# Fewer, wider vector operations, twelve conversion blocks moved forward, and five buffers for split weights in a chunk-attention, expert and MLP kernel

## The chip, the core and the metric

The kernel runs on one core of a Trainium2 chip. Its metric is the device time of one execution in microseconds (us). TensorE is written PE, VectorE DVE, ScalarE ACT, GpSimd POOL and SyncE SP; SP does no arithmetic here and issues all the DMAs, in one queue, in program order.

## The reference, cut to what matters

```python
x = attention over chunks of 64 tokens            # 2304 tokens x 512
P = softmax-like gate of x, 8 Sinkhorn rounds     # 2304 x 8
for e in range(8):                                # experts: 512 -> 1024 -> 512
    h = np.maximum(x @ w1[e], 0.0)
    out += P[:, e:e + 1] * (h @ w2[e])
h = x @ w_in                                      # MLP: 512 -> 2048 -> 512
g = h * np.clip(h + 3.0, 0.0, 6.0) / 6.0
return g @ w_out
```

`w_in` and `w_out` are float64. All else is float32, and the result is wanted in float32 accuracy.

## The kernel before, in words

Each float32 operand is split in two parts, `hi` and `lo` (ACT copies `hi`, POOL subtracts it to leave `lo`), and each product is three PE products: hi·hi, hi·lo, lo·hi. A split is called a **cut** here (`cut_piece`, L804 for ACT and L805 for POOL).

**Phase one** (until 276 us of the profile) holds the attention, the gate and expert 0. It runs over 48 steps (6 blocks of tokens by 8 blocks of hidden units). Each step has four places, called hooks below, at which side work is put into the program (`add(step, hook, ...)`).

**Phase two** holds experts 1 to 7 and the MLP, as two more experts. Its products use a Strassen-like scheme of seven products of half-size blocks in place of eight. The scheme needs sums of the four blocks of each weight matrix. `w1_sum` (L787) and `w2_sum` (L800) make them on DVE, as four operations of 128x256 each, in SBUF; `park_diff`, `x2_diff` and `diff` make such sums of tokens and hidden values. Phase two runs over 108 *slots* of seven *steps* each, a slot being one pair of blocks of hidden units for 768 tokens:

- slots 0 to 27 (276 to 764 us): the first 768 tokens through experts 1 to 7. Here each slot's weights are read, summed and cut for the first time, and the cut parts are stored in DRAM (`wsc`) for the other tokens.
- slots 28 to 83: the other 1536 tokens, with weights read back from `wsc` (`w1_load`, `w2r_load`).
- slots 84 to 107: the MLP. Its weights have to be summed, cut and stored beforehand. `ahead_cut` (cut) and `ahead_keep` (store) do this in two stretches of 56 cuts each, 885 to 1095 us (planned over 87 steps) and 1420 to 1625 us, and `x2_get`, `x2_scale`, `x2_add`, `x2_diff`, `x2_cut`, `x2_keep` prepare the tokens that enter the MLP.

Before all that, `w_in` and `w_out` are turned from float64 into float32 by integer operations, in 32 blocks of 128x512: `cv_load`, seven operations `cv_op` (five on DVE, two on ACT) and `cv_keep`. Before the change the first 23 blocks lie in slots 0 to 27 and 9 in later slots.

In every step the PE does one product into one of three PSUM tiles `ha`, `hb`, `hc`. A product that adds to a tile which has just been read has to wait for the reader: DVE (`u`, `p`: L925) or ACT (`p`: L929). So a late DVE or ACT stops the PE, at most two or three steps later.

What stands in which step is decided while the program is built. `book` puts an operation into the first step in which estimated engine loads (the numbers `dve=`, `act=`, `pool=`) leave room. Every engine executes its operations strictly in that order.

The buffer `m` (one tile per partition row, 4608 floats, reached by `part(offset, size)`) serves in turn for the conversion, for the MLP's weights and for its tokens. In it the cut weights of `ahead_cut` have two places, used by turns:

```python
w = part(2048 + n % 2 * 512, 512, F32R).rearrange("p (a n) -> p a n", a=2)
```

Of the kernel before, what the change touches and what calls it, by code (L numbers as in the profile page):

```python
# [28 lines left out]
def chunk_attention_moe_mlp(  # L29
# [23 lines left out]
    nc = tc.nc  # L53
# [118 lines left out]
    cv_in = {}  # L172
# [6 lines left out]
    def cv_load(i, o):  # L179
        src, _, r, c = cv_list[i]  # L180
        t = part(o, 2 * CW, U32)
        nc.sync.dma_start(
            out=t,
            in_=src.bitcast(U32)[r * 128:(r + 1) * 128, 2 * c * CW:2 * (c + 1) * CW],
        )
        cv_in[i] = t.rearrange("p (n a) -> p n a", a=2)

    CV_COST = (0.5, 0.7, 0.7, 1.1, 0.75, 0.9, 0.9)

    def cv_op(i, n, o):  # L190
        t = cv_in[i]
        lw, hw = t[:, :, 0], t[:, :, 1]
        kx = part(o + 2 * CW, CW, U32)
# [23 lines left out]
    def cv_keep(i, o):  # L217
        _, dst, r, c = cv_list[i]
        nc.sync.dma_start(
            out=dst[r * 128:(r + 1) * 128, c * CW:(c + 1) * CW], in_=part(o + 2 * CW, CW)  # L220
        )
# [216 lines left out]

    def att_x(u):
        t, hh = u  # L440
        ps = at.pop(u)["ps"]
        j, o = divmod(t * 128, NP)
        for c in range(2):
# [251 lines left out]
    PRODUCTS = {1: (1, 0), 2: (2, 1), 3: (6, 2), 4: (0, 6), 5: (3, 3), 6: (4, 4), 7: (5, 5)}  # L695
# [86 lines left out]

    def w1_sum(k, n):
        t = raw1[k]
        o, x, y, op = ((4, 0, 1, ALU.add), (5, 4, 2, ALU.subtract), (6, 2, 0, ALU.subtract),
                       (7, 3, 5, ALU.subtract))[n]
        nc.vector.tensor_tensor(out=t[:, o], in0=t[:, x], in1=t[:, y], op=op)  # L787

    def w2_sum(k, n):
        r = raw2[k]  # L790
        if n == 0:
            if k < NEXP:
                raw2[k, "s"] = pools["sum2"].tile([128, 4, 256], F32, tag="s2", name=f"s2_{k}")
            else:
                raw2[k, "s"] = r[:, 4:8]
        t = raw2[k, "s"]
        A11, A12, A22, A21 = [r[:, o] for o in range(4)]
        o, x, y, op = ((0, A21, A22, ALU.add), (1, t[:, 0], A11, ALU.subtract),
                       (2, A11, A21, ALU.subtract), (3, A12, t[:, 1], ALU.subtract))[n]
# [170 lines left out]
    def h_turned(s, r):  # L970
# [19 lines left out]
        elif r == 6:  # L990
            gate(s, t["p1"], t["p1"], 0)
            first(3)
            put(s, 2, t["p1"])
            squash(s, t["u2"])
        elif r == 7:
            gate(s, t["u2"], t["u2"], 1)
            diff(s, 5, t["t1"], t["u2"], t["t1"])
        elif r == 8:
            diff(s, 7, t["u2"], t["u3"], t["u2"])
        elif r == 9:  # L1000
            diff(s, 6, t["u3"], t["u3"], t["t1"])
# [45 lines left out]
    MW = {1: 4, 2: 5, 3: 3, 4: 6, 5: 0, 6: 1, 7: 2}  # L1047
# [178 lines left out]
    def x2_diff(kl, n):  # L1226
        a, b, c, d = x2t[kl]
        o, x, y = ((b, a, b), (a, c, a), (c, c, b), (d, d, c))[n]
        nc.vector.tensor_tensor(out=o, in0=x, in1=y, op=ALU.subtract)


    def x2_get(p, kl):
        nc.sync.dma_start(
            out=part(0, 2 * NP), in_=xraw[p][:, kl].rearrange("p i j n -> p (i j n)")
        )
        nc.sync.dma_start(
# [4 lines left out]
        a = xf_tiles(0)  # L1241
        x2t[kl] = [a[1], a[0], a[3], a[2]]
# [32 lines left out]
    with tc.manual_schedule():  # L1275
# [12 lines left out]
        opened("x01", "x0", 1, "left")  # L1288
        for p in range(NPAIR):
            xhi[p] = pools[f"x{p}"].tile([128, KD, NP], F32R, tag="xh", name=f"xh{p}")  # L1290
            xlo[p] = pools[f"x{p}"].tile([128, KD, NP], F32R, tag="xl", name=f"xl{p}")
# [130 lines left out]

        def to_right():
# [19 lines left out]
        for n in range(4):  # L1443
# [141 lines left out]
        for s in slots[:TURN]:  # L1585
# [5 lines left out]
            for n in range(4):  # L1591
                g = book(g, w2_sum, s.k, n, dve=0.7)
# [23 lines left out]
        def book_cv(g, todo, bases, pace):  # L1616
            n = len(bases)
            back = [g] * n
            for c, i in enumerate(todo):
                o = bases[c % n]  # L1620
                at_slot(0, back[c % n], cv_load, i, o)
                t = g = max(g, back[c % n] + 4)
                for x, cost in enumerate(CV_COST):
                    act = x in (1, 2)
                    g = book(g, cv_op, i, x, o, dve=cost * (not act), act=cost * act)
                at_slot(0, g + 1, cv_keep, i, o)
                back[c % n] = g + 1
                g = max(g, t + pace)
            return g + 2

        CV1 = 23
        g = book_cv(4, list(range(CV1)), (0, 3 * CW, 6 * CW), 8)
# [17 lines left out]
        def book_ahead(g, todo):  # L1650
# [4 lines left out]
            for u, (k, m) in enumerate(units):  # L1655
                plain, sums = ((0, 1, 2), (3, 4, 5, 6)) if m == 1 else ((4, 5, 6), (0, 1, 2, 3))
                h = g
                for n in range(4):
                    h = book(h, w1_sum if m == 1 else w2_sum, k, n, dve=0.65)
                for n, o in enumerate(plain + sums):  # L1660
                    if n == 3:
                        g = max(g, h + 1)
                        if u + 1 < len(units):
                            fetch(max(g, h + 1), *units[u + 1])
# [99 lines left out]
```

## Time and profile before

| what | value |
|---|---|
| median of 3 runs | 2030.87 us (2024.29 to 2033.15) |
| the profiled execution's own time | 2026.22 us |
| its span, first to last instruction | 2024.4 us |
| mean granted clock of the PE | 0.985 of full speed |
| PE busy | 1926.4 us, 95% of the span |
| DVE busy | 1618.5 us, 80% |
| POOL busy | 1238.4 us, 61% |
| ACT busy | 813.7 us, 40% |

The span is 1.8 us shorter than the execution's own time, which holds the start and the end around it. The profiled execution lies near the lower end of the runs. A granted clock of 1.00 is the PE's 2.4 GHz and 0.5 is 1.2 GHz; a mean between them says for how long the lower one was granted.

### The profile page before, as it was taken

The numbers are of one execution on the slowest core, as the hardware profiler recorded it, in microseconds if no ns is written. First come the engines' busy times: TensorE is split into PE (matmuls) and PEld (weight loads), VectorE is DVE, ScalarE is ACT, GpSimd is POOL, SyncE is SP. The second block draws the span as 40 slices with busy tenths as digits, with TensorE's granted clock in tenths as the row PEclk, the third lists the DMA queues.
The fourth block names the chain that finished last, engine by engine and source line by source line (L and its number), as shares of the span: only waits on it lengthen the run. The fifth ranks groups of instructions, "written<-read, shape, count | busy, mean of one in ns | idle before, by whom it ended". The sixth has DMA issues, their size and how long they took to land.

```text
span 2024.4 us, 34606 instructions
## 1 busy us (share of the span) xinstructions
PE 1926.4 (95%) x11915; PEld 1830.6 (90%) x11915; DVE 1618.5 (80%) x2421; ACT 813.7 (40%) x1636; POOL 1238.4 (61%) x1099
## 2 busy tenths in 40 slices
PE   9999998999999999998999999999989999899998
PEld 8799997878877878998989999999989999899998
DVE  6556578898998976887888999978878877797867
ACT  5223245554545543433333333333333335445453
POOL 3213358787877875766676555667667755555554
PEclk9999999999999999999999999999999999999999
DMA  9865679998987987999999889999999999898884
GB/s 214 205 165 159 244 266 360 312 312 304 311 311 276 326 312 248 339 322 316 319 333 307 291 325 305 324 315 324 320 306 326 341 377 311 305 305 284 304 272 151
DMA packets 354447, 594.59 MB, mean 294 GB/s; under 512 B 56528, under 2 KB 172384, under 8 KB 354144
## 3 DMA queue, kind: packets, MB, share of 16 engines
q1 hardware_dynamic: 354272, 592.37, 86.7%
q8 instruction: 95, 1.56, 0.3%
q14 instruction: 80, 0.66, 0.1%
HBM read 406.08 MB, written 186.20 MB: 293 GB/s over the span
## 4 chain that ended last, share of the span: by engine, by line
PE 59%; DVE 16%; DMA 13%; issue 4%; POOL 4%; ACT 2%; SPq 2%; DVEq 0%; POOLq 0%; ACTq 0%
PE o L1141 13%; PE hb L883 10%; PE o L1131 7%; PE ha L883 6%; PE hc L883 6%; DMA wsc<-m 6%; PE h L571 5%; PE acc L608 5%; DVE r L787 4%; DVE s L800 3%; PE acc L1023 3%; DMA W2R<-wsc 2%; DVE u L925 2%; DMA x2sc<-m 1%; POOL m L805 1%
## 5 line engine op out<-in xcount | busy, mean ns | idle before, releaser
L883 PE MATMUL hb<-X,W 128*128 128x384 f32 x1560 | 321.0, 340 | 34.3 <-DVE u L925 34.1
L883 PEld LDWEIGHTS hb<-X,W 128*128 128x128 f32 x1560 | 274.0, 190 | 50.9 <-DVE u L925 46.5
L1141 PE MATMUL o<-Hb,W2R 128*128 128x384 f32 x1296 | 280.0, 338 | 9.7 <-POOL Hb L805 7.5
L1023 PE MATMUL acc<-W,H 128*128 128x512 f32 x1008 | 264.5, 397 | 0.9 <-POOL H L906 0.6
L883 PE MATMUL hc<-X,W 128*128 128x384 f32 x1200 | 245.1, 339 | 1.1 <-DVE H L900 0.8
L1141 PEld LDWEIGHTS o<-Hb,W2R 128*128 128x128 f32 x1296 | 232.5, 190 | 11.9 <-POOL Hb L805 8.7
L1166 DVE SCALAR_TENSOR_TENSOR accM<-o,accM 128x768 f32<-128x768 f32 x209 | 199.0, 952 | 46.8 <-PE o L1141 31.5
L805 POOL TENSOR_TENSOR W<-r,W 128x512 fp32r<-128x512 f32 (+1 forms) x166 | 220.2, 1357 | 23.0 <-ACT W L804 23.0
L1141 PE MATMUL o<-Ha,W2R 128*128 128x384 f32 x1056 | 228.6, 336 | 0.0
L883 PEld LDWEIGHTS hc<-X,W 128*128 128x128 f32 x1200 | 212.7, 191 | 9.9 <-DVE H L900 3.8
L1023 PEld LDWEIGHTS acc<-W,H 128*128 128x128 f32 x1008 | 190.5, 191 | 32.4 <-POOL H L906 4.3
L805 POOL TENSOR_TENSOR Hb<-u,Hb 128x384 fp32r<-128x384 f32 x144 | 161.9, 1128 | 90.9 <-ACT Hb L804 70.7
L883 PE MATMUL ha<-X,W 128*128 128x384 f32 x912 | 188.6, 342 | 26.2 <-ACT p L929 22.6
L883 PEld LDWEIGHTS ha<-X,W 128*128 128x128 f32 x912 | 161.5, 191 | 32.8 <-ACT p L929 25.0
L1141 PEld LDWEIGHTS o<-Ha,W2R 128*128 128x128 f32 x1056 | 188.4, 189 | 0.0
L925 DVE TENSOR_TENSOR u<-hb,p 128x384 f32<-128x384 f32 x216 | 118.7, 550 | 74.4 <-ACT p L929 36.4
L805 POOL TENSOR_TENSOR m<-m 128x256 fp32r<-128x256 f32 x112 | 98.1, 876 | 89.5 <-ACT m L804 82.0
L805 POOL TENSOR_TENSOR Ha<-t,Ha 128x384 fp32r<-128x384 f32 x89 | 98.1, 1103 | 79.9 <-ACT Ha L804 78.3
L805 POOL TENSOR_TENSOR Hb<-p,Hb 128x384 fp32r<-128x384 f32 x94 | 109.1, 1161 | 57.7 <-ACT Hb L804 38.6
L805 POOL TENSOR_TENSOR Ha<-u,Ha 128x384 fp32r<-128x384 f32 x96 | 110.7, 1154 | 50.7 <-ACT Ha L804 46.1
L925 DVE TENSOR_TENSOR u<-hc,u 128x384 f32<-128x384 f32 x216 | 118.5, 548 | 29.0 <-PE hc L883 28.8
L1131 PE MATMUL o<-W2R,Hb 128*128 128x256 f32 x837 | 130.9, 284 | 5.9 <-DMA W2R<-wsc 5.9
(189 smaller groups left out, 3907.2 us busy)
## 6 DMA issues: line engine op xcount, KB each, us to landing
W2R<-wsc SPq DMA_DIRECT2D x280, 512.0 KB, 5.5
W<-wsc SPq DMA_DIRECT2D x504, 256.0 KB, 5.4
wsc<-W SPq DMA_DIRECT2D x28, 1792.0 KB, 7.3
wsc<-SS SPq DMA_DIRECT2D x28, 1024.0 KB, 8.2
wsc<-m SPq DMA_DIRECT2D x112, 256.0 KB, 4.9
r<-in_moe_w_dram SPq DMA_DIRECT2D x84, 256.0 KB, 8.0
wsc<-W SPq DMA_DIRECT2D x28, 768.0 KB, 8.2
x2sc<-m SPq DMA_DIRECT2D x42, 384.0 KB, 5.6
```

Of the source, the lines that this page charges most:

```text
L571: nc.tensor.matmul(out=hps[:, :n], lhsT=w[:, a, kk, :], rhs=xx[:, kk, :], start=(kk == 0 and a == 0 and xx is xh), stop=(kk == KD - 1 and ...
L608: nc.tensor.matmul(out=o, lhsT=w[:, a, c] if turned else hx[:, c], rhs=hx[:, :n] if turned else w[:, a, :], start=(f == 0 and hx is hi and ...
L787: nc.vector.tensor_tensor(out=t[:, o], in0=t[:, x], in1=t[:, y], op=op)
L800: nc.vector.tensor_tensor(out=t[:, o], in0=x, in1=y, op=op)
L805: lo_eng.tensor_tensor(out=lo, in0=r, in1=hi.bitcast(F32), op=ALU.subtract)
L883: nc.tensor.matmul(out=ps[:, :HN], lhsT=W1t[s.b][:, wo, a, kl, :], rhs=x[:, b, kl, :], start=(start and kl == 0 and a == 0 and b == 0), st ...
L925: nc.vector.tensor_tensor(out=o, in0=ps[b][:, :HN], in1=x, op=ALU.add)
L1023: nc.tensor.matmul(out=o, lhsT=s.Hs[:, fi, hx, t * 128:(t + 1) * 128], rhs=w[:, 0::3, a, :] if fi == 0 else w[:, 1:3, a, :], start=(s.j % ...
L1131: nc.tensor.matmul(out=o[:, t * 256:(t + 1) * 256], lhsT=hs[q][:, b, t * 128:(t + 1) * 128], rhs=w[:, q, a, :], start=(q, a, b) == mm[0] a ...
L1141: nc.tensor.matmul(out=ps[:, d, :HN], lhsT=w[:, q, a, d * 128:(d + 1) * 128], rhs=hs[q][:, b, :], start=(q, a, b) == mm[0] and not again, ...
L1166: nc.vector.scalar_tensor_tensor(out=dst, in0=src, scalar=sc, in1=dst, op0=ALU.mult, op1=ALU.add)
```

## The change

**Sums.** The seven sums of a scheme are formed in three operations in place of four. The first makes two 128x256 results at once, as one operation of 128x512 whose second operand is the same block for both; the other two are 128x256. Signs of two of the intermediate results change, and the tables `PRODUCTS` and `MW` follow. For token and hidden-value sums the count stays at four a set; one of the four becomes `minus_both`, which subtracts and negates in one operation.

**Conversion.** Twelve blocks move into phase one, one at a time, every eight hooks, with two places of a new buffer `cv` by turns. The other 20 are converted in pairs: one operation covers 128x1024. Seven pairs lie in slots 0 to 27, and three after the first stretch of `ahead_cut`. Room for `cv` comes from the tokens of the third 768-token group, which now take over the place of the first group (`x_new`).

**Buffers.** The cut MLP weights get five places in `m` in place of two.

**Order.** The tokens for the MLP are fetched by two functions: `x2_first` (the part that is known early) and `x2_get`; some distances and estimated costs in the planner change.

```diff
-    def cv_load(i, o):
-        src, _, r, c = cv_list[i]
-        t = part(o, 2 * CW, U32)
-        nc.sync.dma_start(
...
+    def cv_load(ii, o):
+        for n, i in enumerate(ii):
+            src, _, r, c = cv_list[i]
+            nc.sync.dma_start(
+                out=part(o + n * 2 * CW, 2 * CW, U32),
...
+    def cv_op(ii, n, o):
+        w = len(ii) * CW
+        t = part(o, 2 * w, U32).rearrange("p (n a) -> p n a", a=2)
...
     def w1_sum(k, n):
         t = raw1[k]
-        o, x, y, op = ((4, 0, 1, ALU.add), (5, 4, 2, ALU.subtract), (6, 2, 0, ALU.subtract),
-                       (7, 3, 5, ALU.subtract))[n]
+        if n == 0:
+            nc.vector.tensor_tensor(
+                out=t[:, 4:6], in0=t[:, 1:3],
+                in1=t[:, 0:1].to_broadcast([128, 2, 2, 128]), op=ALU.subtract,
+            )
+            return
+        o, x, y, op = ((6, 4, 2, ALU.add), (7, 3, 6, ALU.subtract))[n - 1]
         nc.vector.tensor_tensor(out=t[:, o], in0=t[:, x], in1=t[:, y], op=op)
...
-        w = part(2048 + n % 2 * 512, 512, F32R).rearrange("p (a n) -> p a n", a=2)
+        w = part(2048 + n % 5 * 512, 512, F32R).rearrange("p (a n) -> p a n", a=2)
...
+        CV0 = 12
+
+        def cv_early(at0, pace):
+            for i in range(CV0):
+                q, o = at0 + i * pace, i % 2 * 3 * CW
+                add(0, q - 7 if i > 1 else at0 - 6, cv_load, (i,), o)
+                for x, y in enumerate((0, 2, 2, 4, 5, 6, 7)):
+                    add(0, q + y, cv_op, (i,), x, o)
+                add(0, q + 8, cv_keep, (i,), o)
+
+        cv_early(4 * pos[0, 1, 1] + 2, 8)
...
-        CV1 = 23
-        g = book_cv(4, list(range(CV1)), (0, 3 * CW, 6 * CW), 8)
+        CV1 = 26
+        g = book_cv(2, list(range(CV0, CV1)), 0, 25)
...
         for p in (1, 2):
-            g = max(g + 2, 7 * ends[p] + 23)
+            g = max(g + 2, 7 * ends[p] + 17)
             for kl in range(2):
-                at_slot(0, g, x2_get, p, kl)
-                g += 5
+                at_slot(0, g, x2_first, p, kl)
+                h = max(g + 1, 7 * ends[p] + 26)
+                at_slot(0, h, x2_get, p, kl)
+                g += 8
```

The PE executes the same instructions in the same order before and after. Three places show what moves elsewhere.

The first is DVE in slots 5 and 6 (`u_5`, `p_5`, `u_6` are the readers of PSUM on which the PE waits; `r` and `s` are the weight blocks and their sums; `m` is the conversion). Before:

```order
L787 TENSOR_TENSOR r_7_4382<-r_7_4382 128x256
L205 SCALAR_TENSOR_TENSOR m<-m 128x512
L925 TENSOR_TENSOR p_5_4433<-hb_4457,p_5_4433 128x384
L208 TENSOR_SCALAR m<-m 128x512
L211 SCALAR_TENSOR_TENSOR m<-m 128x512
L925 TENSOR_TENSOR u_5_4464<-hc_4524,u_5_4464 128x384
L214 SCALAR_TENSOR_TENSOR m<-m 128x512
L800 TENSOR_TENSOR s_6_4593<-r_6_4444 128x256
L800 TENSOR_TENSOR s_6_4593<-s_6_4593,r_6_4444 128x256
L800 TENSOR_TENSOR s_6_4593<-r_6_4444 128x256
L800 TENSOR_TENSOR s_6_4593<-r_6_4444,s_6_4593 128x256
L925 TENSOR_TENSOR u_6_4618<-hb_4611,p_6_4587 128x384
```

After, at the same place:

```order
L957 TENSOR_TENSOR p_5_4516<-hb_4537,p_5_4516 128x384
L204 SCALAR_TENSOR_TENSOR m<-m 128x1024
L207 TENSOR_SCALAR m<-m 128x1024
L957 TENSOR_TENSOR u_5_4544<-hc_4603,u_5_4544 128x384
L210 SCALAR_TENSOR_TENSOR m<-m 128x1024
L826 TENSOR_TENSOR s_6_4670<-r_6_4526 128x512
L832 TENSOR_TENSOR s_6_4670<-s_6_4670,r_6_4526 128x256
L832 TENSOR_TENSOR s_6_4670<-r_6_4526,s_6_4670 128x256
L957 TENSOR_TENSOR u_6_4691<-hb_4684,p_6_4664 128x384
```

Four sums in a row ahead of the PSUM reader `u_6` have become three, of which the first is twice as wide; the conversion's operations are twice as wide and stand in fewer slots.

The second is DVE in phase one, at the first steps of the second token block (`hl` is the expert's hidden value, `ex`, `mx`, `sm`, `rs` the attention's softmax). After the change:

```order
L592 SCALAR_TENSOR_TENSOR hl_1_1_1110<-h_1_1_1091,hh_1_1_1109 128x512
L195 TENSOR_SCALAR cv<-cv 128x512
L464 TENSOR_TENSOR xl_177<-pv_6_None,xh_176 128x4x64 x2
...
L393 RECIPROCAL rs_None<-sm_None 128x8
L204 SCALAR_TENSOR_TENSOR cv<-cv 128x512
L207 TENSOR_SCALAR cv<-cv 128x512
L308 STREAM_TRANSPOSE qT_None<-q_None 128x128 x4
L308 STREAM_TRANSPOSE kT_None<-k_None 128x128 x4
L210 SCALAR_TENSOR_TENSOR cv<-cv 128x512
```

None of the `cv` rows stood there before; the rows around them are the same. The one that waits for a DMA is the first (L195).

The third is SP's queue where the second half of the last 768 tokens is fetched for the MLP (`W2R` are weights that the PE needs soon, `X` and `XE` tokens for the next slots, `x2sc` stores out of `m`). Before:

```order
L1221 DMA x2sc_124<-m 128x2x384
L1233 DMA m<-xraw_118 128x1536
L1236 DMA m<-asc_t_127 128x2x768
L1267 DMA m<-ptd 128x6x128
L1079 DMA W2R<-wsc_17_115 128x1024
```

After:

```order
L1253 DMA x2sc_124<-m 128x2x384
L756 DMA X_3162<-x2sc_123 128x1536
L1111 DMA W2R<-wsc_17_115 128x1024
L756 DMA X_3162<-x2sc_123 128x1536
L756 DMA XE<-x2sc_123 128x1536
L1270 DMA m<-asc_t_127 128x2x768
L1299 DMA m<-ptd 128x6x128
L1111 DMA W2R<-wsc_17_115 128x1024
L1263 DMA m<-xraw_118 128x1536
```

The load of `asc_t` into `m`, which needs the store ahead of it to be done, has moved behind four other DMAs, one of them a `W2R`.

## Rows read from the trace of the kernel before

**Rows 1.** Busy time by stretch: us, engines (instructions), PE clock, DMA share, GB/s
```profile
0.00:276.00 276.00, 271.77 (x2479) 243.82 (x2480) 160.40 (x433) 88.91 (x190) 82.61 (x83) 1.00 0.72 199
276.00:764.00 488.00, 450.88 (x2155) 393.56 (x2155) 425.14 (x542) 253.40 (x498) 382.25 (x301) 0.98 0.90 314
...
885.00:1095.00 210.00, 188.38 (x1035) 185.87 (x1034) 174.85 (x246) 69.55 (x160) 146.01 (x143) 0.95 0.95 320
1095.00:1420.00 325.00, 323.31 (x1860) 321.79 (x1859) 287.41 (x401) 110.30 (x212) 193.54 (x172) 1.00 0.91 315
1420.00:1625.00 205.00, 191.81 (x1077) 190.33 (x1077) 167.57 (x239) 68.84 (x158) 144.91 (x145) 0.98 0.95 325
1625.00:2024.00 399.00, 384.14 (x2660) 381.96 (x2658) 311.53 (x434) 177.91 (x332) 212.69 (x193) 0.99 0.84 288
```

**Rows 2.** PE's longest wait in stretch two, three, five, six of Rows 1: total, times, longest
```profile
PE hb L883 <- DVE u L925: 31.5, 23, 3.7
...
PE ha L883 <- ACT p L929: 20.9, 6, 7.2
...
PE ha L883 <- ACT p L929: 9.0, 2, 6.6
...
PE o L1131 <- DMA W2R<-wsc: 5.9, 2, 4.9
```

**Rows 3.** DVE's weight sums, groups by line, 276 to 764 us: busy, mean ns
```profile
L787 DVE TENSOR_TENSOR r<-r 128x256 f32<-128x256 f32 x104 | 105.5, 1034 | 0.9
L800 DVE TENSOR_TENSOR s<-r 128x256 f32<-128x256 f32 x56 | 61.0, 1089 | 4.4 <-DMA r<-in_moe_w_dram 4.4
L800 DVE TENSOR_TENSOR s<-r,s 128x256 f32<-128x256 f32 x28 | 33.4, 1195 | 0.0
L800 DVE TENSOR_TENSOR s<-s,r 128x256 f32<-128x256 f32 x28 | 31.9, 1141 | 1.0
```

**Rows 4.** Busy time at tile m alone (conversion), 276 to 764 us: PE, PEld, DVE, ACT
```profile
276.00:764.00 488.00, 0.00 (x0) 0.00 (x0) 98.57 (x115) 32.86 (x46) 0.00 (x0) 0.98 0.90 314
```

**Rows 5.** Timeline of DVE and PE about one stall: start, us, [idle before]
```profile
346.50 1.37 DVE L800 TENSOR_TENSOR s<-s,r 128x256 f32<-128x256 f32 x1
...
349.31 0.54 DVE L925 TENSOR_TENSOR u<-hb,p 128x384 f32<-128x384 f32 x1
...
349.91 0.69 PE L883 MATMUL hb<-X,W 128*128 128x384 f32 x1 [3.70 <-DVE u L925]
```

**Rows 6.** ACT's longest wait, 885 to 1095 us, then 1420 to 1625 us
```profile
ACT m L804 <- DMA wsc<-m: 83.8, 37, 5.6
...
ACT m L804 <- DMA wsc<-m: 77.3, 34, 7.1
```

**Rows 7.** Timeline of ACT and PE about another stall
```profile
936.74 0.42 ACT L804 ACTIVATE m<-m 128x256 fp32r<-128x256 f32 x1 [5.62 <-DMA wsc<-m]
...
940.22 0.47 ACT L929 ACTIVATE p<-ha 128x384 f32<-128x384 f32 x1
...
940.74 0.69 PE L883 MATMUL ha<-X,W 128*128 128x384 f32 x1 [7.24 <-ACT p L929]
```

**Rows 8.** SP's wait for a store at 1749 to 1757 us, and the PE behind it
```profile
SPq L1236 <- DMA x2sc<-m: 8.4, 1, 8.4
...
1767.33 2.26 PE L1131 MATMUL o<-W2R,Hb 128*128 128x256 f32 x9 [4.91 <-DMA W2R<-wsc]
```

**Rows 9.** Single lines, whole span: duration ns min/median/max
```profile
L787 DVE TENSOR_TENSOR r<-r x112: 407/1046/1522, 238.0 to 725.8; 128x256 f32<-128x256 f32 x112
...
L214 DVE SCALAR_TENSOR_TENSOR m<-m x32: 674/692/1664, 318.1 to 1264.8; 128x512 f32<-128x512 f32 x32
...
L805 POOL TENSOR_TENSOR SS<-s,SS x56: 1268/1472/1562, 283.9 to 756.9; 128x512 fp32r<-128x512 f32 x56
```

**Rows 10.** DMA issues, whole span: count, KB each, us to landing
```profile
wsc<-m SPq DMA_DIRECT2D x112, 256.0 KB, 4.9
...
m<-in_moe_w_in_dram SPq DMA_DIRECT2D x16, 512.0 KB, 5.9
```

**Rows 11.** SP's longest wait in phase one, 50 to 276 us
```profile
SPq L669 <- POOL xc L666: 65.1, 14, 14.9
```

More of the change, by code (lines that the diff above doesn't have):

```diff
@@ L215, in cv_op, with cv_keep @@
                 op0=ALU.mult, op1=ALU.mult)
[L217 to L221, printed above, removed]
+    def cv_keep(ii, o):
+        for n, i in enumerate(ii):
+            _, dst, r, c = cv_list[i]
+            nc.sync.dma_start(
+                out=dst[r * 128:(r + 1) * 128, c * CW:(c + 1) * CW],
+                in_=part(o + 2 * len(ii) * CW + n * CW, CW),
+            )
     HH = H // 2
@@ L442, in att_x @@
         j, o = divmod(t * 128, NP)
+        if j not in xhi:
+            x_new(j)
         for c in range(2):
@@ L796, in w2_sum @@
         t = raw2[k, "s"]
-        A11, A12, A22, A21 = [r[:, o] for o in range(4)]
-        o, x, y, op = ((0, A21, A22, ALU.add), (1, t[:, 0], A11, ALU.subtract),
-                       (2, A11, A21, ALU.subtract), (3, A12, t[:, 1], ALU.subtract))[n]
+        if n == 0:
+            nc.vector.tensor_tensor(
+                out=t[:, 0:2], in0=r[:, 0:3:2],
+                in1=r[:, 3:4].to_broadcast([128, 2, 256]), op=ALU.subtract,
+            )
+            return
+        o, x, y, op = ((2, t[:, 1], r[:, 0], ALU.add), (3, r[:, 1], t[:, 2], ALU.subtract))[n - 1]
         nc.vector.tensor_tensor(out=t[:, o], in0=x, in1=y, op=op)
@@ L1287, in chunk_attention_moe_mlp @@
         opened("x01", "x1", 1, "left")
[L1288 to L1291, printed above, removed]
+        opened("x01", "cv", 1, "left")
+        M["m"] = pools["cv"].tile([128, 6 * CW], F32, tag="cv", name="cv")
+        for p in range(2):
+            x_new(p)
         opened("edge", "edge", 1, "right")
@@ L1442, in chunk_attention_moe_mlp @@
             add(s + 1, 1 + 4 * n, load_X, 0, n)
-        for n in range(4):
+        for n in range(NSUM):
             add(s + 4, n, w1_sum, 0, n)
@@ L1614, in chunk_attention_moe_mlp, with book_cv @@
             at_slot(3, t, acc_scale, 0, t)
[L1616 to L1622, printed above, removed]
+        def book_cv(g, todo, o, pace):
+            while todo:
+                ii = tuple(todo[:2])
+                del todo[:2]
+                t = g
+                at_slot(0, g, cv_load, ii, o)
+                g += 4
                 for x, cost in enumerate(CV_COST):
                     act = x in (1, 2)
[L1625 to L1628, printed above, removed]
+                    if x in (1, 3):
+                        g += 2
+                    cost = (cost + 0.45) * len(ii) / 2
+                    g = book(g, cv_op, ii, x, o, dve=cost * (not act), act=cost * act)
+                at_slot(0, g + 1, cv_keep, ii, o)
+                g = max(g + 1, t + pace)
             return g + 2
-        CV1 = 23
-        g = book_cv(4, list(range(CV1)), (0, 3 * CW, 6 * CW), 8)
+        CV1 = 26
+        g = book_cv(2, list(range(CV0, CV1)), 0, 25)
         assert g < 7 * TURN + 5, g
```

86 lines of the change are left out of this document (48 added, 38 removed).

## The prediction

> **What bounds the kernel now.** I read the busy times by stretch first, because the PE is busy 95% of the span and executes the same instructions after the change: only its idle time and its clock can give anything. In each stretch the loss is span minus PE busy time, plus the share by which the granted clock is below 1.00 [rows 1]:
>
> - slots 0 to 27 (276 to 764 us): idle 488 − 450.9 = 37.1 us; clock 0.02 × 488 = 9.8 us.
> - first `ahead_cut` stretch (885 to 1095 us): idle 21.6, clock 0.05 × 210 = 10.5.
> - second (1420 to 1625 us): idle 13.2, clock 0.02 × 205 = 4.1.
> - the MLP (1625 to 2024 us): idle 14.9, clock 4.0.
> - phase one: idle 4.2. And 1095 to 1420 us: idle 1.7.
>
> All stretches together lose some 98 us idle and 30 us of clock (0.015 of the span). Then I read who ended the waits [rows 2]. In slots 0 to 27 it is DVE, late with `u` (23 waits, 31.5 us). In both `ahead_cut` stretches it is ACT, late with `p` (20.9 and 9.0 us). In the MLP it is a `W2R` load (5.9 us). So there are three different causes, and each has an edit in the change that touches it.
>
> Why is DVE late in slots 0 to 27? It is busy 425 of 488 us there [rows 1], and the timeline shows the pattern: three sums and more stand directly ahead of `u`, which starts at 349.31 us, and the PE has then waited 3.70 us [rows 5]. Why is ACT late? At 936.74 us it has waited 5.62 us for a store out of `m`, since the next cut reuses one of only two places; `p` stands behind it in ACT's order, is done at 940.69, and the PE has waited 7.24 us [rows 7]. ACT spends 83.8 and 77.3 us of the two stretches in that one wait [rows 6].
>
> **The change, part by part.**
>
> *Sums in slots 0 to 27.* 216 operations cost 105.5 + 61.0 + 33.4 + 31.9 = 231.8 us, 1.073 us each, so a set of four costs 4.29 us [rows 3]. The shortest one took 0.407 us [rows 9]; so on average 0.67 us of each is waiting inside the operation. The new 128x512 sum is not in the trace. The shortest 128x512 operation of DVE there took 0.674 us [rows 9]. Lower bound: 0.67, no waiting. Upper bound: 2 × 1.073 = 2.15, waiting that grows with the length, and then a set still costs 4.29. I take one wait an operation: 0.67 + 0.67 = 1.34, because the wait (0.67) is larger than the work (0.41) even in the short ones and all share the same POOL neighbours. A set then costs 1.34 + 2 × 1.07 = 3.49, 0.80 less; 54 sets give 43 us of DVE time (bounds 0 and 79).
>
> What is that wait? The 128x256 sums spread from 407 to 1522 ns, and POOL's subtractions of 128x512 take at least 1268 ns [rows 9]: 407 + 1268 is 1675, near the upper end. The Trainium skill (SBUF — State Buffer, section "Who interferes with whom") says that DVE with two SBUF inputs and GpSimd share a port pair as an exclusive lock, and the later one fully blocks; the trace agrees in the spread. By that rule the wider sums also hold the lock longer against POOL, which speaks against the change; what it would give is the second rival below.
>
> *Conversion in slots 0 to 27.* 115 operations took 98.6 us, 0.857 each [rows 4]. 14 blocks in pairs are 35 operations of 128x1024, again not in the trace. From 256 to 512 columns the shortest time grows by 0.674 − 0.407 = 0.267 us [rows 9]; 512 columns more make 0.53, so 0.857 + 0.53 = 1.39 each, 49 us together, 50 us less (bounds: 0.857 and 1.71 each, 69 and 39 us less).
>
> Together DVE falls from 425 to about 332 us, against some 441 us that the PE needs there (450.9 busy less the clock loss): 75% in place of 87%. A neighbour shows that this is enough: from 1095 to 1420 us DVE was busy 88% and the PE idle for 1.7 us only [rows 1]. What stops the PE are bursts, and a burst stays in each slot, shorter by 0.80 us, in most slots without a conversion (0.86 us) ahead of it. The mean wait was 31.5 / 23 = 1.37 us; I leave 0.3 for each, 7 us, and 1.5 us of the other idle time there. The gain is 37.1 − 8.5 = 28.6 us and most of the clock loss, since it follows the stalls: 8 of 9.8. **Sum: 36.5 us.**
>
> *Five places for cut weights.* The first stretch took 210 us for 87 planned steps, of which 32 us were lost: 178 / 87 = 2.05 us a step. The new plan puts the 56 cuts into 81 steps, one every 3.0 us. With two places a store has under 6 us from issue to reuse, and its median landing is 4.9 us [rows 10] with waits to 7.1 us beyond that [rows 6]. With five it has some 15 us. So ACT's wait goes, and with it 20.9 + 9.0 us of PE waits. What is late next? The DMA engines are busy 0.95 in both [rows 1]; shorter stretches ask for more GB/s, so I leave 6 us of loads that come late. Gain 24 us idle, and 11 of the 14.6 us of clock. **Sum: 35 us.**
>
> *Fetch in two parts.* SP waited 8.4 us at the load of `asc_t` for a store just issued, and the `W2R` load behind it made the PE wait 4.91 us [rows 8]. After the change four DMAs and three steps lie between, 6 us of the 8.4. I count 5 us idle and 2 of the 4.0 us of clock: **7 us.**
>
> *Phase one.* 60 DVE operations at 0.857 are at most 51 us, on an engine busy 160 of 276 us: 76%, so the cover is there. ACT gets 24 operations (32.86 / 46 = 0.71 us each [rows 4]), 17 us on 89. The cuts that the PE waits for keep their place ahead of them. DMA share there is 0.72. I charge 1.5 us, for a delayed reader now and then; the dangerous case is a rival.
>
> The token sums stay as many; the shared place of the first and third token group is free long before it is wanted: its last reader stands at the end of block 1, the first writer some 30 hooks later.
>
> **Sum.** Against the profiled execution's own 2026.2 us: 2026.2 − 36.5 − 35 − 7 + 1.5 = 1949. The median of before lay 4.6 us above that execution; I predict 1950 for the median after.
>
> **The rivals.**
>
> 1. *DMA becomes the bound in the two `ahead_cut` stretches.* Stores no longer hold ACT back, and loads of `W` and `W2R` come late. With the engines busy all the time the same bytes take 210 × 0.95 = 199.5 and 205 × 0.95 = 195 us. The gain there would be 20 us in place of 35: **1964**. For it: the shares. Against: conversion leaves the first stretch, and the loads are asked for up to a slot ahead.
> 2. *The wider operations wait as long as the lock rule allows.* Each 128x512 sum meets a whole POOL subtraction: 0.67 + 1.27 = 1.94, a set costs 4.09, and the 54 sets save 11 us in place of 43. DVE then falls to 364 us and bursts are hardly shorter; about half of 36.5 us comes: **1967**. The rule is that of the Trainium skill's page named above. Against it: by the mean, the short sums waited 0.67, about half of that.
> 3. *The buffers do nothing for the PE.* ACT waits for the next late thing in its order, and `p` stays late: only 36.5 + 7 − 1.5 comes, **1984**. Against: in those rows the store is ACT's longest wait in both stretches [rows 6].
> 4. *Slower: loads for the conversion come late in phase one.* The first `cv` operation waits for its load on DVE, ahead of readers that the PE needs. It is asked for seven hooks ahead; 276 us over 192 hooks are 1.4 us a hook, 10 us, and landing takes 5.9 [rows 10]. But SP has waited up to 14.9 us for POOL there [rows 11]. If each of 12 blocks cost the PE more than 77 / 12 = 6.4 us, nothing is left; at 8 us the time is 1949 + 96 = **2045**. Against: the PE idles 4.2 us in the whole of phase one although SP waits like that, as a queue does that runs ahead.
>
> **How the numbers follow.** The forecast gets 0.64, with its own range of 1930 to 1962: at the low end stand the lower bounds, with no burst and no late load left (8.5 + 6 us and the rest of the clock, some 20 us less), at the high end two thirds of the bursts' gain. Rival 1 gets 0.14, rival 2 0.10, rival 3 0.06, rival 4 0.06, of which 0.04 cost more than all gains and 0.02 about as much. The range of 8 in 10 reaches over the first three rivals, 1928 to 1985. A change under 0.5% (10 us) can't be told from none here; a further 0.01 goes there from rival 3. Faster 0.93, same 0.03, slower 0.04.
>
> **What would show it.** PE waits for `u` in slots 0 to 27 fall from 31.5 to under 12 us, and the 128x512 sum takes about 1.34 us (0.67 or 2.15 would move rival 2). ACT's wait for stores out of `m` falls under 15 us in both stretches, and the PE's for `p` with it; if waits for `W` or `W2R` stand there instead, rival 1 holds. The clock reads 0.99 or more over the span. SP's 8.4 us falls below 3. In phase one, no wait for `cv`. I am wrong if stalls of the same length return behind another engine, or if phase one grows by more than 5 us.

## The result, and the profile after

After the change the median is **1940.31 us** (1938.06 to 1943.21, 4 runs) against 2030.14 us of before (4 runs): a ratio of 0.956 (95% interval 0.954 to 0.959). The profiled execution took 1938.06 us, with a span of 1936.3 us at a mean granted clock of 0.997 (before 0.985). The forecast was 1950 us in a range of 1928 to 1985.

The stretches are cut where the first product of slot 0 starts and where the first product on `XE` tokens (slot 28) starts:

| | phase one | slots 0 to 27 | the rest | span |
|---|---|---|---|---|
| before | 276.2 | 487.7 | 1260.5 | 2024.4 |
| after | 286.6 | 446.7 | 1203.0 | 1936.3 |
| difference | +10.4 | −41.0 | −57.5 | −88.1 |
| forecast | +1.5 | −36.5 | −35 and −7 | −77 |

Busy time of the changed kernel by stretch, in the columns of [rows 1] (length, PE, PEld, DVE, ACT, POOL, granted clock, DMA share, GB/s); the two `ahead_cut` stretches are the fourth and sixth row:

```profile
0.00:286.00 286.00, 274.72 (x2476) 245.89 (x2477) 202.25 (x491) 105.18 (x213) 87.69 (x83) 0.99 0.79 225
286.00:733.00 447.00, 436.52 (x2156) 388.83 (x2155) 336.48 (x408) 237.98 (x466) 394.26 (x301) 1.00 0.94 325
733.00:868.00 135.00, 133.07 (x762) 130.69 (x760) 101.72 (x151) 49.69 (x98) 85.49 (x76) 1.00 0.89 306
868.00:1039.00 171.00, 171.00 (x988) 171.00 (x988) 149.81 (x213) 65.09 (x150) 141.26 (x138) 1.00 0.99 362
1039.00:1372.00 333.00, 332.43 (x1918) 332.11 (x1917) 289.41 (x398) 111.42 (x210) 201.09 (x175) 1.00 0.92 317
1372.00:1543.00 171.00, 171.00 (x989) 171.00 (x988) 152.87 (x212) 65.55 (x152) 141.66 (x138) 1.00 0.99 366
1543.00:1936.00 393.00, 379.41 (x2638) 377.26 (x2636) 309.62 (x429) 177.26 (x330) 211.09 (x191) 0.99 0.84 289
```

In both `ahead_cut` stretches the PE is now never idle. In slots 0 to 27 it idles 447 − 436.5 = 10.5 us instead of 37.1, with DVE busy 336 of 447 us instead of 425 of 488. Only phase one got worse: 11.3 us idle instead of 4.2. Over the span the PE is busy 1898.1 us instead of 1926.4 and idle 38.2 instead of 98.0, which is the whole difference of 88.1. The PE's longest waits over the whole span (total, times, longest) answer to [rows 2]:

```profile
PE hb L915 <- DVE u L957: 6.2, 7, 1.6
PE acc L1055 <- POOL H L938: 4.9, 5, 2.2
PE sc_None L343 <- DVE xl L464: 4.1, 4, 1.7
PE o L1173 <- DVE u L993: 2.5, 1, 2.5
PE pv_None L431 <- ACT aT_None L412: 2.2, 1, 2.2
PE sc L357 <- ACT kT L323: 1.4, 2, 0.7
PE o L1173 <- DMA W2R<-wsc: 1.3, 1, 1.3
```

The 31.5 us for `u` in slots 0 to 27 are now 6.2 over the whole span, 2.9 of them in slots 0 to 27; the wait for ACT's `p` behind a store is gone. The third and fifth row are new and lie in phase one. DVE's weight sums in slots 0 to 27 (busy, mean ns), and its conversion there (the busy columns are PE, PEld, DVE, ACT, POOL), answer to [rows 3] and [rows 4]:

```profile
L815 DVE TENSOR_TENSOR r<-r 128x256 f32<-128x256 f32 x52 | 63.7, 1226 | 1.6
...
L809 DVE TENSOR_TENSOR r<-r 128x512 f32<-128x512 f32 x26 | 30.3, 1164 | 0.0
L832 DVE TENSOR_TENSOR s<-r,s 128x256 f32<-128x256 f32 x28 | 30.2, 1079 | 0.9
...
L826 DVE TENSOR_TENSOR s<-r 128x512 f32<-128x512 f32 x28 | 30.2, 1078 | 3.0 <-POOL SS L837 3.0
L832 DVE TENSOR_TENSOR s<-s,r 128x256 f32<-128x256 f32 x28 | 25.1, 898 | 1.0
...
286.00:733.00 447.00, 0.00 (x0) 0.00 (x0) 49.37 (x35) 15.96 (x14) 0.00 (x0) 1.00 0.94 325
```

The 128x512 sums took 1.16 and 1.08 us, no longer in the mean than the 128x256 ones beside them (119.0 us for 108, 1.10 each). 54 sets cost 179.5 us, 3.32 each, against 4.29.

What a sum waits for can be read by setting it against the POOL operation that runs when it starts. One wide and one narrow sum (start, us):

```profile
429.08 1.34 POOL L938 TENSOR_TENSOR H<-u,H 128x384 fp32r<-128x384 f32 x1 [0.62 <-ACT H L937]
429.47 1.50 DVE L826 TENSOR_TENSOR s<-r 128x512 f32<-128x512 f32 x1
...
462.39 1.14 POOL L938 TENSOR_TENSOR H<-u,H 128x384 fp32r<-128x384 f32 x1 [0.28 <-ACT H L937]
462.69 1.12 DVE L832 TENSOR_TENSOR s<-s,r 128x256 f32<-128x256 f32 x1
```

The wide one ends 0.55 us after POOL's operation, the narrow one 0.28. In slots 0 to 27 of this trace 89 of the 108 narrow sums started while a POOL operation ran, and all 89 ended about 0.28 us after its end (169 of 173 before the change); the other 19 took 0.42 us. Of the 54 wide ones 48 started so, and 40 of them ended about 0.55 us after it (of the other eight five took 0.68 us, as if nothing held them, and three 1.54 to 1.88); the six that met none took 0.68. So a sum waits as a rule once, for what is left of POOL's operation, whatever its own width. The wider sum does cost some 0.26 us more work. Its mean is as short as the narrow one's because of where it stands: it found 0.58 us of a POOL operation left in the mean of its 48 cases, the narrow ones 0.97 us in their 89.

New stalls in phase one, in the timeline of DVE, ACT and PE (start, us, [idle before and what ended it]):

```profile
136.34 0.43 DVE L195 TENSOR_SCALAR cv<-cv 128x512 uint32<-128x512 uint32 x1 [3.92 <-DMA cv<-in_moe_w_in_dram]
136.80 0.72 ACT L198 ACTIVATE cv<-cv,three 128x512 f32<-128x512 uint32 x1 [5.69 <-DVE cv L195]
137.56 0.72 ACT L201 ACTIVATE cv<-cv,three 128x512 uint32<-128x512 f32 x1
138.18 0.58 ACT L412 ACTIVATE aT_None<-at_None 128x512 f32<-128x512 f32 x1
...
138.81 0.98 PE L431 MATMUL pv_None<-aT_None,v 64*64 64x64 f32 x32 [2.22 <-ACT aT_None L412]
...
210.15 0.72 ACT L201 ACTIVATE cv<-cv,three 128x512 uint32<-128x512 f32 x1
211.15 0.65 ACT L463 ACTIVATE xh<-pv_None 128x256 fp32r<-128x256 f32 x2
211.75 0.74 DVE L464 TENSOR_TENSOR xl<-pv_None,xh 128x256 fp32r<-128x256 f32 x2
...
212.22 1.30 PE L343 MATMUL sc_None<-kT_None,qT_None 64*64 64x64 f32 x32 [1.72 <-DVE xl L464]
```

At 136 us DVE stood idle for 3.9 us until the block's load had landed, ACT's two conversion operations stood behind it, and behind those the copy `aT` for which the PE waited. At 210 us no load is late: two conversion operations of 0.72 us stand ahead of `xh`, `xl` follows, and the PE waits for it.

### The profile page after: what moved, and what is told of

Its sections match the earlier page's. It is cut to its first block, busy times and chain, and to the rows that moved or that the text cites. A ratio compares the mean times of both kernels' runs of the same rounds, so it can differ in the third digit from the quotient of the medians.

```text
span 1936.3 us, 34426 instructions
## 1 busy us (share of the span) xinstructions
PE 1898.1 (98%) x11915; PEld 1816.8 (94%) x11915; DVE 1542.2 (80%) x2299; ACT 812.2 (42%) x1616; POOL 1262.5 (65%) x1099
## 4 chain that ended last, share of the span: by engine, by line
PE 80%; DVE 8%; DMA 4%; POOL 3%; issue 2%; ACT 2%; SPq 1%; DVEq 0%; POOLq 0%; ACTq 0%
PE o L1173 21%; PE hb L915 15%; PE hc L915 9%; PE ha L915 9%; PE o L1163 8%; PE acc L1055 6%; PE h L579 4%; PE acc L616 4%; POOL W L837 2%; DMA W2R<-wsc 1%; DMA r<-in_moe_w_dram 1%; DVE r L815 1%; POOL H L938 1%; PE sc_None L343 1%; POOL SS L837 1%
## 5 line engine op out<-in xcount | busy, mean ns | idle before, releaser
L915 PE MATMUL hb<-X,W 128*128 128x384 f32 x1560 | 315.3, 336 | 5.9 <-DVE u L957 5.6
L915 PEld LDWEIGHTS hb<-X,W 128*128 128x128 f32 x1560 | 272.7, 188 | 13.9 <-DVE u L957 7.3
L1173 PE MATMUL o<-Hb,W2R 128*128 128x384 f32 x1296 | 276.1, 335 | 5.0 <-DVE u L993 2.5
L915 PE MATMUL ha<-X,W 128*128 128x384 f32 x912 | 183.5, 335 | 1.2 <-DVE p L957 1.2
L836 ACT ACTIVATE Hb<-u 128x384 fp32r<-128x384 f32 x144 | 75.6, 525 | 158.9 <-DVE u L667 49.3
```

The source lines that it names most:

```text
L836: nc.scalar.activation(out=hi, in_=r, func=AF.Copy)
L915: nc.tensor.matmul(out=ps[:, :HN], lhsT=W1t[s.b][:, wo, a, kl, :], rhs=x[:, b, kl, :], start=(start and kl == 0 and a == 0 and b == 0), st ...
L1173: nc.tensor.matmul(out=ps[:, d, :HN], lhsT=w[:, q, a, d * 128:(d + 1) * 128], rhs=hs[q][:, b, :], start=(q, a, b) == mm[0] and not again, ...
```

## The experiments

The theory: each term is worth what undoing its edit gives back, the whole gain being PE idle time and the clock that goes with it; the growth of phase one comes from the early blocks. The rival readings: the gain of the rest comes from the conversion's removal from the `ahead_cut` stretches and not from the places; pairing and fewer sums are hidden beside the PE; phase one grew by the token sums or the shared token place. Each run below is the changed kernel with one edit, unless it says otherwise; stretches are of its one profiled execution, which can lie at either end of the run's range.

| run | phase one | slots 0 to 27 | rest | median (runs' range) | ratio to before |
|---|---|---|---|---|---|
| `two_places` | 286.7 | 446.9 | 1234.4 | 1974.75 (1969.79 to 1983.68) | 0.974 [0.971, 0.978] |
| `two_along` | 287.5 | 447.4 | 1248.1 | 1982.53 (1981.18 to 1984.77) | 0.977 [0.976, 0.979] |
| `four_sums` | 285.6 | 460.6 | 1204.3 | 1952.40 (1949.02 to 1955.72) | 0.963 [0.960, 0.965] |
| `slot_singles` | 286.5 | 456.7 | 1206.5 | 1951.17 (1950.71 to 1955.07) | 0.962 [0.961, 0.963] |
| `late_singles` | 277.1 | 475.7 | 1205.9 | 1956.34 (1953.39 to 1960.51) | 0.964 [0.963, 0.966] |
| `none_early` | 276.7 | 498.4 | 1200.3 | 1979.57 (1977.18 to 1980.08) | 0.976 [0.974, 0.978] |
| `fetch_at_once` | 284.3 | 447.4 | 1204.2 | 1939.99 (1935.41 to 1942.81) | 0.956 [0.954, 0.958] |
| `early_light` | 281.0 | 445.8 | 1203.3 | 1931.29 (1929.49 to 1932.28) | 0.952 [0.950, 0.954] |
| `early_three` | 283.3 | 447.0 | 1201.0 | 1934.96 (1933.09 to 1937.28) | 0.954 [0.952, 0.955] |
| `early_aligned` | 280.1 | 448.9 | 1204.9 | 1935.23 (1932.05 to 1938.02) | 0.954 [0.952, 0.955] |

Six of these ten have the changed kernel's own instructions in the rest (all but the first three and `fetch_at_once`), and it took them 1200.3 to 1206.5 us: a difference of a few us in the rest can't be put down to an edit. Phase one varies as well: the changed kernel and the four runs that leave it as it is (`two_places`, `two_along`, `slot_singles`, `fetch_at_once`) took 284.3 to 287.5 us for it.

**Five places back to two.**

```diff
-        w = part(2048 + n % 5 * 512, 512, F32R)...
+        w = part(2048 + n % 2 * 512, 512, F32R)...
```

> The changed kernel with two places in place of five for the cut MLP weights; nothing else. If the five places are what took ACT's wait away, then that wait (out of m, for stores) returns with 50 us or more in each ahead stretch, the PE waits for p again with 20 to 30 us in all, the clock loses about 8 to 10 us beside it, and the time is 1965 to 1980 us. If the shorter DVE work and the conversion moved behind the first stretch are what helped there, the time stays within 1940 to 1950 us.

The rest grew by 31.4 us, and nothing else moved. By the medians the run is 34.4 us longer. ACT's longest wait and the PE's, from 733 us on, are those of [rows 6] and [rows 2] again:

```profile
ACT m L836 <- DMA wsc<-m: 184.1, 81, 6.5
...
PE ha L915 <- ACT p L961: 21.3, 11, 5.4
```

**Two places, and the last six blocks converted one by one beside the cuts**, as before.

```diff
-        g = book_ahead(g + 4, range(NEXP, NEXP + NG4))
-        g = book_cv(g, list(range(CV1, len(cv_list))), 0, 0)
+        h = book_ahead(g + 4, range(NEXP, NEXP + NG4))
+        g = max(h, book_old(g + 4, list(range(CV1, len(cv_list))), (6 * CW,), 0))
```

> The changed kernel with two places for cut weights, and the last six blocks converted singly alongside the first ahead stretch, in a place of their own, as before the change. Two places alone made the part after slot 27 longer by 31 us (1234 in place of 1203 us), of the 57 us that the change took off there. If conversion alongside is a good part of the other 26 us (ACT, on its way to p, waits for DVE, which waits for a load), this part is 1242 to 1255 us and the total 1983 to 1996 us. If not, it stays at 1232 to 1238 us, total 1972 to 1979 us.

The rest grew by a further 13.7 us in the profiled executions. DVE's `u` operations come in the same order in every kernel, so that two executions can be set beside each other by them. Against the changed kernel the run with two places falls behind by 15.6 us in the first `ahead_cut` stretch and 14.5 in the second. This run falls a further 14 us behind by the end of the first stretch, in which four of its six blocks lie. The PE's wait for `p` there, in `two_places` and in this run:

```profile
PE ha L915 <- ACT p L961: 9.2, 5, 3.6
...
PE ha L915 <- ACT p L961: 14.7, 6, 4.5
```

But the profiled execution is the shortest of the four of the one run and the longest of the other's, the medians are 7.8 us apart and the ranges overlap. That the conversion's company costs time is likely; how much isn't settled.

**Four sums a set again.** The first operation is written as two.

```diff
-            nc.vector.tensor_tensor(out=t[:, 4:6], in0=t[:, 1:3],
-                in1=t[:, 0:1].to_broadcast([128, 2, 2, 128]), op=ALU.subtract)
+            for z in range(2):
+                nc.vector.tensor_tensor(out=t[:, 4 + z], in0=t[:, 1 + z], in1=t[:, 0], op=ALU.subtract)
```

> The changed kernel with the 128x512 first sum issued as two 128x256 operations, so four operations a set again, at the same places. If an operation waits about once whatever its length (the wide one took 1.10 us, a narrow one 1.04 to 1.17), DVE gets about 1 us more a set, 54 us in slots 0 to 27, bursts ahead of u are as long as before the change, and the PE waits there rise by 10 to 25 us: 1952 to 1970 us. If waits grow with the length, DVE time and total stay: 1936 to 1945 us.

Slots 0 to 27 grew by 13.9 us. Busy times there (columns as above) and the PE's wait for `u`, which was 2.9 us in this stretch after the change:

```profile
286.00:746.00 460.00, 441.23 (x2150) 387.97 (x2149) 371.52 (x461) 236.80 (x465) 384.68 (x301) 0.99 0.91 316
...
PE hb L911 <- DVE u L953: 6.8, 6, 1.9
...
PE hc L911 <- DVE u L953: 4.1, 4, 1.3
```

DVE worked 35 us more, 0.65 us for each of the 54 added operations, and 14 of it reached the path.

**The 14 blocks of slots 0 to 27 one by one** through three places (`book_old` is the planner's loop of before).

```diff
-        g = book_cv(2, list(range(CV0, CV1)), 0, 25)
+        g = book_old(2, list(range(CV0, CV1)), (0, 3 * CW, 6 * CW), 12)
```

> The changed kernel with its 14 blocks of slots 0 to 27 converted one by one through three places, as before, in place of seven pairs. If pairing is worth what the durations of the rows say, seven blocks' worth of small operations more stand on DVE (about 9 to 11 us), slots 0 to 27 take 452 to 457 us and the total is 1944 to 1951 us. If DVE has room for it beside the PE (336 of 447 us busy), slots 0 to 27 stay within 3 us of 447 and the total at or below 1943 us.

Slots 0 to 27 grew by 10.0 us. The conversion's DVE time there (tile `m` alone), all busy times, and the wait:

```profile
287.00:743.00 456.00, 0.00 (x0) 0.00 (x0) 64.02 (x70) 19.93 (x28) 0.00 (x0) 0.99 0.92 319
...
287.00:743.00 456.00, 437.91 (x2150) 390.93 (x2149) 346.89 (x442) 240.28 (x479) 376.99 (x301) 0.99 0.92 319
...
PE hb L915 <- DVE u L957: 14.2, 8, 2.8
```

The same blocks cost 64.0 us in place of 49.4, and PE waits for `u` of up to 2.8 us are back although DVE is busy only 76% of the stretch. In the two longest of these waits five DVE operations, 6.2 us of work, stand in a row ahead of `u`: one of the conversion, three sums and one on `acc`. What counts here is how long the work ahead of `u` is, not the share. The run doesn't part the width of the operations from the steps at which they stand, since the planner places singles otherwise than pairs.

**No block in phase one: 26 blocks one by one in slots 0 to 27.**

```diff
-        CV0 = 12
+        CV0 = 0
...
-        g = book_cv(2, list(range(CV0, CV1)), 0, 25)
+        g = book_old(2, list(range(CV0, CV1)), (0, 3 * CW, 6 * CW), 7)
```

> The changed kernel with no conversion in phase one, 26 single blocks in slots 0 to 27 with three places by turns, as the kernel before had 23. Unlike the run with 13 pairs in one place, DVE should not wait for loads here. Phase one goes back to 277 us. DVE in slots 0 to 27 gets 26 x 4.29 = 112 us of conversion in place of 49, some 398 of 447 us (89%). If DVE at that share holds the PE up in bursts, the slots take 460 to 475 us and the total is 1943 to 1960 us. If 89% is no limit, they stay under 455 us and the total is 1930 to 1938 us: then the move into phase one was a loss.

Against `slot_singles` the slots grew by 19.0 us and phase one shrank by 9.4: the move of twelve blocks trades the second for the first. With no early block phase one is 277.1 us, 0.9 us above that of before, so the shared token place and the token sums cost nothing that can be told from none. DVE is the nearly full engine again (411 of 476 us), and the PE waits for it:

```profile
277.00:753.00 476.00, 442.80 (x2156) 389.02 (x2155) 411.20 (x503) 256.15 (x504) 390.37 (x301) 0.99 0.95 325
...
PE ha L915 <- DVE p L957: 20.6, 16, 1.7
```

**No block in phase one, 26 blocks in 13 pairs.** To fit them in, a pair's operations follow its load by three steps in place of four.

```diff
-        CV0 = 12
+        CV0 = 0
...
-                g += 4
+                g += 3
...
-        g = book_cv(2, list(range(CV0, CV1)), 0, 25)
+        g = book_cv(2, list(range(CV0, CV1)), 0, 0)
```

> The changed kernel with no conversion in phase one: 26 blocks as 13 pairs in slots 0 to 27. If the twelve early blocks are what made phase one longer, its end (the first product of slot 0) goes back from 286 to 277 us. DVE in slots 0 to 27 gets 60 more column blocks, 6 pairs of five operations at about 1.3 us, 40 us, and is then busy some 375 of 447 us; by the bursts the PE waits there rise by 5 to 15 us. The total is then 1932 to 1948 us, near no difference: the move was worth little. If DVE in those slots is at its limit again, they get 20 us or more longer and the total is above 1955 us.

The time falls in the second range named, above 1955 us, but not for its reason: DVE is busy 372 of 498 us in slots 0 to 27 and not at its limit. With one place for a pair and less lead, DVE waits for the conversion's loads there, and the PE behind it. The run says nothing about pairs; `late_singles` and `slot_singles` took its place.

```profile
DVE m L195 <- DMA m<-in_moe_w_out_dram: 32.8, 5, 7.4
DVE m L195 <- DMA m<-in_moe_w_in_dram: 32.3, 6, 8.0
...
PE hc L915 <- DVE H L932: 33.3, 9, 4.7
```

**The fetch in one piece again**, in the planner:

```diff
-                at_slot(0, g, x2_first, p, kl)
-                h = max(g + 1, 7 * ends[p] + 26)
-                at_slot(0, h, x2_get, p, kl)
-                g += 8
+                at_slot(0, g, x2_get, p, kl)
+                at_slot(0, g, x2_first, p, kl)
+                g += 5
```

> The changed kernel with the MLP tokens fetched all at once and at the old distances, as before the change. If the earlier fetch of the known part is what took SP's 8.4 us wait and the PE's 4.9 us wait for W2R away, both come back near the start of the MLP, with 2 to 3 us of clock: 1946 to 1952 us. If other edits had already taken them away, the time stays at 1938 to 1943 us.

Missed: the total is the same. The waits of [rows 8] did come back (first fence: SP and PE of this run from 1540 us on), but the changed kernel has other waits at the start of the MLP (second fence: PE of the changed kernel from 1543 us on):

```profile
SPq L1270 <- DMA x2sc<-m: 8.0, 1, 8.0
...
PE o L1163 <- DMA W2R<-wsc: 5.0, 2, 4.4
```

```profile
...
PE o L1173 <- DVE u L993: 2.5, 1, 2.5
PE o L1173 <- DMA W2R<-wsc: 1.3, 1, 1.3
```

They don't stand at the same place. The start of the MLP in this run and in the changed kernel, then the stretch with the fetch in this run and in the changed kernel, each pair cut at the same two `u` operations (columns as above):

```profile
1544.80:1574.60 29.80, 29.80 (x174) 29.80 (x173) 23.08 (x35) 10.26 (x20) 13.70 (x15) 1.00 1.02 397
...
1543.70:1579.40 35.70, 31.88 (x174) 31.30 (x173) 23.16 (x35) 10.26 (x20) 14.39 (x16) 0.95 0.98 375
...
1655.50:1683.70 28.20, 23.46 (x156) 22.97 (x155) 18.11 (x28) 10.47 (x20) 12.59 (x12) 0.95 0.89 334
...
1659.20:1680.90 21.70, 21.32 (x152) 21.12 (x151) 15.82 (x25) 10.08 (x20) 12.26 (x12) 1.00 1.02 379
```

At its own place the edit is worth 28.2 − 21.7 = 6.5 us. The changed kernel loses 5.9 us at the start of the MLP, some 100 us earlier, which this run doesn't lose. Whether the edit brings that loss is open: `two_along`, which has the fetch in two parts, took 30.3 us there, `late_singles`, which has it too, 35.8, and the kernel before, without it, 31.8.

**Early blocks nearly without work.** Six of the seven operations are left out, so that the twelve blocks are loaded and stored but not converted.

```diff
-                for x, y in enumerate((0, 2, 2, 4, 5, 6, 7)):
-                    add(0, q + y, cv_op, (i,), x, o)
+                add(0, q, cv_op, (i,), 0, o)
```

> The changed kernel, which leaves out six of the seven operations of the twelve early blocks: load, first DVE operation and store stay, the other four DVE and two ACT operations are not done. If the longer phase one comes from DVE waiting for the loads (3.9 us once), it stays at 284 to 286 us. If it comes from the time of the DVE and ACT operations ahead of the readers of PSUM, it goes back to 278 to 280 us and the total to 1932 to 1934 us.

Phase one fell by 5.6 us, to 281.0, between the two ranges named, which is still 4.3 above `none_early`. So six of the seven operations account for a little over half of the growth, and the loads, the first operation's wait for them and the stores for the other part.

**Three places for the early blocks**, so that a load is asked for 15 hooks ahead in place of 7.

```diff
-                q, o = at0 + i * pace, i % 2 * 3 * CW
-                add(0, q - 7 if i > 1 else at0 - 6, cv_load, (i,), o)
+                q, o = at0 + i * pace, i % 3 * 3 * CW
+                add(0, q - 15 if i > 2 else at0 - 6, cv_load, (i,), o)
```

> The changed kernel with three places in place of two for the early conversion, and each load asked for 15 hooks ahead in place of 7. Leaving out six of the seven operations gave back 5.6 of the 10.4 us by which phase one is longer; the rest may be the loads. If DVE's waits for loads (6.7 us in all) are the other part, they go, phase one ends at 281 to 283 us and the total is 1934 to 1937 us. If it is DMA traffic or the remaining operations, phase one stays at 285 to 287 us and the total at 1939 to 1942 us.

**Three places, and the operations put beside the unit's own** (the unit's `starts` in place of an even pace).

```diff
+            qs = [starts[0] + 4] + starts[1:]
+            for i, q in enumerate(qs):
...
+                for x, y in enumerate((1, 3, 3, 4, 5, 5, 6) if q < late else (2, 4, 4, 5, 6, 7, 8)):
```

> The changed kernel with three places for the early blocks and their seven operations put at steps of an attention unit at which neither the copies of the scores nor the split of x stand (a table of starts in place of an even pace). If what is left of the growth of phase one, beside late loads, is the conversion's ACT and DVE operations standing ahead of the unit's own, phase one falls from the 283.3 us of three places alone to 278 to 281 us and the total to 1928 to 1933 us. If the growth is only the engines' added work wherever it stands, phase one stays at 282 to 285 us and the total at 1933 to 1938 us.

Phase one from 50 us on, of four kernels, one fence each: the changed one, `early_three`, `early_aligned`, `late_singles`:

```profile
50.00:286.00 236.00, 228.81 (x1873) 205.03 (x1872) 168.67 (x411) 79.37 (x159) 72.01 (x65) 0.99 0.75 228
```

```profile
50.00:283.00 233.00, 228.23 (x1880) 204.74 (x1879) 169.28 (x411) 80.09 (x161) 72.52 (x65) 1.00 0.77 231
```

```profile
50.00:280.00 230.00, 227.73 (x1879) 204.50 (x1880) 166.11 (x412) 79.87 (x161) 70.48 (x65) 1.00 0.78 234
```

```profile
50.00:277.00 227.00, 226.98 (x1881) 204.24 (x1880) 127.18 (x352) 63.66 (x137) 66.82 (x65) 1.00 0.66 195
```

The PE idles 7.2, 4.8, 2.3 and 0.0 us (6.7 to 8.9 in the four runs with the same phase one): of 7.2 us late loads account for some 2.4 and the order on ACT and DVE for some 2.5, and the last 2.3 stay without a name. In length the growth over `late_singles` is 9.5 us; `early_three` lies only 1.0 us below the shortest phase one of those runs, so that its share of the growth is less sure than the idle time. Its median is below that of the changed kernel (1934.96 against 1940.31 us, no run of the one inside the other's range), but the intervals of their ratios to before meet. `early_aligned` met its expectation in phase one and missed it in the total: 1.9 us went in the slots and 3.9 in the rest, which is within the spread named above.

## Why the prediction was right, and where it was off

The sign and the two large causes held. The total came 10 us below the forecast, by errors that in part cancel: the gains of the slots and of the two `ahead_cut` stretches were sized too small, the price of phase one too.

- **Slots 0 to 27, −36.5 forecast, −41.0 measured.** Undoing the sums gives back 13.9, undoing the pairs 10.0, and moving the twelve blocks back on top of that 19.0, 42.9 together. The wide sum was sized at 1.34 us and took 1.12 (60.5 us for 54). One wait an operation was the right step: the trace shows it as the rest of the POOL operation that runs. Its size, 0.67 us, was a mean over narrow sums; the wide one's work of 0.68 leaves 0.44. That it met less of POOL's work than the narrow ones was not foreseen and is luck. A set fell by 0.97 in place of 0.80. The pair's operation took 1.41 us (forecast 1.39), DVE's total 336 us (332), the PE's idle time 10.5 us (8.5), and its waits for `u` are below the 12 us named.
- **Five places, −35 forecast.** The cause is shown: `two_places` brings back ACT's wait and 31.4 us of the rest. The forecast left 6 us of late loads besides other idle time; the PE's idle time in both stretches is 0. That DMA engines at a share of 0.95 would be late was the wrong step: at 0.99 they moved 362 and 366 GB/s in place of 320 and 325.
- **The rest as a whole, −42 forecast, −57.5 measured.** Set beside the changed kernel by the `u` operations, the kernel before loses 29.0 us in the first `ahead_cut` stretch and 18.5 in the second, 6.8 from slot 28 to the first stretch, and 3.3 in all else. Two places bring back 15.6 and 14.5 of the two stretches. What no term had is the conversion beside the cuts, which the first rival named only in passing: in the first stretch `two_along` adds some 14 us, about what is missing there, though the medians of the whole times are only 7.8 us apart. Of the nine late blocks of before three were finished in that stretch, and the others stood behind it, where the PE idled 1.7 us. The 4 us left in the second stretch and the 6.8 ahead of the first have no experiment.
- **Fetch, −7 forecast, about 0 in the total.** The long wait went (SP's from 8.4 to 1.7 us), and at its place the count "5 us idle and 2 of clock" held: 6.5 us against `fetch_at_once`. But at the start of the MLP the changed kernel takes 5.9 us more than that run and 3.9 more than the kernel before, so that the PE's idle time in the MLP fell only from 14.9 to 13.6 us. The forecast had no term for that, and its cause is open.
- **Phase one, +1.5 forecast, +10.4 measured.** The step that failed is "76%, so the cover is there". DVE's share was no higher than that (202 of 286 us, 71%), and the loads mostly came in time (DVE waited twice, 6.7 us in all), but in phase one the PE waits for single ACT and DVE operations in a chain, and an operation of 0.7 us ahead of such a reader delays it. The text's own sign for an error, growth of over 5 us, did appear. Rival 4's mechanism is real at a small size: 0.8 us a block and not 6.4, and late loads are some third of it.
- **Rivals 1 to 3** are refuted: 1 by the full PE at a DMA share of 0.99, 3 by `two_places`. Rival 2 asked for 1.94 us for a wide sum, and it took 1.12. It was worked out from the rule that DVE with two SBUF inputs and GpSimd exclude each other and the later one fully blocks (the Trainium skill, SBUF — State Buffer, "Who interferes with whom"); the trace agrees with the rule, as all 89 narrow sums that started beside a POOL operation ended behind it, but not with the step of the rival that each wide sum meets a whole POOL operation: what was left of it was 0.58 us in the mean. That the spread of DVE's sums comes from POOL was only argued in the forecast, and this trace shows it.

## What to carry to other kernels

Judge room on an engine by the work that stands in a row ahead of a reader for which the PE waits, and not by its busy share: work moved onto an engine at 76% cost 9.5 us, and pairs of operations at 75% still gained 10. When work that shares a stretch with a bottleneck moves away, give that stretch a term of its own. If a buffer's release is on the path, count the time from issue to reuse against the landing: five places in place of two were worth 31 us, and with a third place for the early blocks the PE's idle time in phase one was 4.8 us in place of 7.2. Where a DVE operation waits for a POOL operation, fewer and wider operations save waits: each of the 54 operations less was worth 0.65 us of DVE time.

## What the runs showed of the hardware

- A DVE sum of two operands in SBUF that started while a POOL operation ran ended about 0.28 us after that operation's end for 128x256 (89 of 89 after the change, 169 of 173 before) and about 0.55 us after it for 128x512 (40 of 48). With no POOL operation running they took 0.42 and 0.68 us. In these cases the wait is for the rest of one POOL operation, whatever the width.
- The DMA engines moved 320 GB/s at a share of 0.95 before and 362 to 366 at 0.99 after, with the landing of the cuts' stores at a median of 5.9 us in place of 4.9. A share near 1 is not yet a full engine.
- The granted clock followed the stalls: 0.95 in the first `ahead_cut` stretch of before, where the PE idled 21.6 of 210 us, and 1.00 after, where it never did. From slot 28 on, PE busy time for the same instructions fell from 1203.8 to 1186.9 us.
